# Token-mixing tails as two row tiles inside the next batch's score group, in a fused pooling attention and MLP-mixer kernel on Trainium2

## The chip, the cores and the metric

The kernel runs on one core of one Trainium2 chip. The metric is the device time of one execution in microseconds (us), given as the median of several runs. The engines are named as in the profile: PE is the matrix engine TensorE (PEld its weight loads), DVE is VectorE, ACT is ScalarE, POOL is GpSimd, SP is SyncE, which here only issues transfers.

## The reference

Inputs are q, k, v of 8 batches, 8 heads, 576 positions and 64 channels, and four weight matrices. What is computed, cut to what matters:

```python
k_p = k.reshape(B, H, Sp, pool, D).mean(axis=3)      # pool = 8, Sp = 72 keys
v_p = v.reshape(B, H, Sp, pool, D).mean(axis=3)
attn = softmax(q @ k_p.T / sqrt(D))
x = (attn @ v_p) as [B, 576, 512]
h = relu(x.T @ w_tok1) @ w_tok2                       # token mixing, 576 -> 256 -> 576
u = x + h.T
out = u + relu(u @ w_ch1) @ w_ch2                     # channel mixing, 512 -> 1536 -> 512
```

The kernel takes and gives float32; products are made in bf16.

## The kernel before, in words

The program is written as steps of batches (`2.s0` is step `s0` of batch 2) and units. A unit is the channel mixing of one batch's first 512 positions: unit n holds `l1_tile` (line 517: 12 tiles of four 512-column products, each emptied by a relu on ACT into `GT`, line 521) and then seven products of 12 matmuls with 256 columns (line 583), which a Strassen-like scheme makes out of sums of `GT` and `w_ch2` on DVE (`=1` to `=4`, lines 545 and 557; `w0` to `w3` once for the weights). There are nine units, one for each batch and a ninth for the remaining 64 positions (the tails) of all batches.

A unit yields 45 times: step numbers 0 to 23 lie after each two products of 512 columns, 24 to 44 after each four of 256 columns. The dictionary `PLAN[n]` says which steps of which batches are put in at each of these places, and so fixes the order on all engines: every engine works through its instructions in the order in which they are written. Up to the first unit the list `HEAD` does the same.

The steps of a batch b, with their lines:

- `lk`, `lq`, `lv`: loads of k, q and v, issued from the POOL queue (lines 118 and 128).
- `K0`, `K1`, `V0`, `V1`: pooling of k and v on POOL, three adds each (lines 174 to 180); `v1` is the same on DVE.
- `kpT`: four transposes of the pooled k on PE and a copy to `kD` on ACT (lines 222 and 224). `Q0`, `Q1`: transposes of q on DVE into `qD` (line 284).
- `s0`, `s1`, `s2`: a score group (`scores`, lines 297 and 306). The heads' products have 32 channels a piece, so four of them stand side by side on PE as 32-row tiles; two exponentials on ACT follow. `s0` and `s1` make 384 positions of one half of the heads each, `s2` the last 192 positions of all heads. They take both of the `p2` PSUM tiles.
- `av0` to `av4`: attention times pooled v, eight products (line 379), then a reciprocal and a multiplication on DVE (lines 383 and 384). `av0` to `av3` give 128 positions each into `x`, `av4` the last 64 into `xt`. An `xt` tile is shared by the two batches of a pair, batch 2i in its upper 64 rows and batch 2i+1 in its lower ones; `w_tok1` therefore stands with the tail's 64 rows twice, each time with zeros in the other half.
- `at0`, `at1`: the first token-mixing product, five products of 512 columns for each half of the 256 hidden rows (line 393), then a relu on ACT (line 395). The fifth product is that of the tail, with 64 of its 128 rows zero.
- `u0` to `u3`: the second token-mixing product and the residual, added on DVE (lines 415 and 416); `u4`: the tails of a pair of batches together (line 410), as one DVE add of 128 rows.
- `t0` to `t3` (PE), or `M0`, `M2`, `M4` (to DRAM), `M`, `MT` (back) and `T0` to `T5` (DVE transposes, line 458), bring `u` into the layout that the next unit needs.
- `g`: a gate (lines 716 and 717). DVE writes a flag and POOL copies it, so that POOL's later steps wait for DVE to come to that place; the next gate's write waits for the copy of the one before.

PSUM has four single banks (`p1a` to `p1d`), which `take` hands out in the order in which they were given back, and two double ones (`p2`). A product that takes a bank waits until its last content was read.

Of the kernel before, what the change touches and what calls it, by code (L numbers as in the profile page):

```python
# [8 lines left out]
FP32 = mybir.dt.float32  # L9
BF16 = mybir.dt.bfloat16  # L10
# [25 lines left out]
def kernel(  # L36
# [72 lines left out]
    exps = [singles.tile([SP, H * S + BP], BF16, name=f"ex{i}") for i in range(2)]  # L109
# [77 lines left out]
    def batch_steps(b):  # L187
# [101 lines left out]
        def scores(i):  # L289
            def go():  # L290
# [9 lines left out]
                exv = st["ex"][:, 0:H * S].rearrange("j (g a l n) -> j a l g n", g=2, a=2, l=2)  # L300
                for a in range(2):
# [23 lines left out]
        def avh(g, c):  # L325
            def go():
# [460 lines left out]
```

## Time and profile before

| | |
|---|---|
| time, median of 3 runs | 264.54 us (263.89 to 265.03) |
| profiled execution, its own time | 264.03 us |
| its span | 262.2 us |
| granted PE clock over the span | 1.00 |
| busy: PE, PEld | 255.8 us (98%), 160.4 us (61%) |
| busy: DVE, ACT, POOL | 179.7 us (69%), 119.2 us (45%), 150.0 us (57%) |
| DMA | 34.29 MB in 31704 packets, mean 131 GB/s |
| chain that ended last, by engine | PE 80%, POOL 8%, DMA 7%, DVE 3% |

The profile was taken from one execution. Its span runs from the first to the last instruction of the program. Groups of instructions are told by line, engine, operation and the tiles written and read. Ends of matmuls are modelled, so that a PE that shows no idle time may still have stood for a fraction of a microsecond; start times are measured. From the starts of the products of line 517, units 0 to 4 begin at 24.2, 56.5, 85.8, 113.5 and 143.8 us.

### The profile page before, as it was taken

What the parts mean: (1) busy time and instruction counts of PE and PEld (TensorE: products, weight loads), DVE (VectorE), ACT (ScalarE), POOL (GpSimd) and SP (SyncE); (2) the same over time, 40 slices, a digit from 0 to 9 for tenths busy, and PEclk for the clock granted to TensorE, in tenths of its full rate; (3) what the DMA queues carried; (4) which work ended last, traced back from release to release, by engine and by line L of the source; (5) the groups of instructions that cost most, each with busy time, mean ns of one, the idle gap of its engine ahead of it and who ended that gap; (6) DMA issues with size and microseconds to landing.
All of it is one profiled execution on the core that took longest, in us unless ns stands there. A gap on an engine that the chain in (4) does not pass through costs nothing.

```text
span 262.2 us, 5324 instructions
## 1 busy us (share of the span) xinstructions
PE 255.8 (98%) x2121; PEld 160.4 (61%) x2121; DVE 179.7 (69%) x370; ACT 119.2 (45%) x195; POOL 150.0 (57%) x177
## 2 busy tenths in 40 slices
PE   8899999999999999999999999999999999999994
PEld 3775556754658545864487448744774486486483
DVE  4566489998786657993899449964795486175183
ACT  2445754149465554435641584155535502612610
POOL 8576145999989999999939881988000000101000
PEclk9999999999999999999999999999999999999999
DMA  7999999992096839699357840831414054503204
GB/s 150 191 200 205 206 206 208 207 223 77 2 172 101 133 118 201 146 196 261 66 154 125 239 133 2 162 92 41 123 35 127 5 158 113 129 0 88 75 0 160
DMA packets 31704, 34.29 MB, mean 131 GB/s; under 512 B 3136, under 2 KB 23744, under 8 KB 31680
## 3 DMA queue, kind: packets, MB, share of 16 engines
q0 software_dynamic: 17632, 17.64, 42.6%
q1 hardware_dynamic: 13632, 15.93, 20.4%
q10 hardware_dynamic: 416, 0.39, 0.5%
q8 instruction: 16, 0.26, 0.4%
q14 instruction: 8, 0.07, 0.1%
HBM read 38.99 MB, written 12.58 MB: 197 GB/s over the span
## 4 chain that ended last, share of the span: by engine, by line
PE 80%; POOL 8%; DMA 7%; DVE 3%; issue 1%; POOLq 0%
PE p1d L517 9%; PE p1c L517 9%; PE p1a L517 8%; PE p1b L517 7%; PE p1b L583 7%; PE p1c L583 7%; PE p1a L583 6%; DMA qb<-in_q_dram 5%; PE p1d L583 4%; PE p L297 3%; PE p L379 3%; POOL t L174 2%; POOL t L175 2%; DMA kr<-in_k_dram 2%; PE p L583 2%; PE p1d L393 2%
## 5 line engine op out<-in xcount | busy, mean ns | idle before, releaser
L717 POOL COPY flag<-flag 1x1 f32<-1x1 f32 x47 | 12.6, 269 | 94.5 <-DVE flag L716 94.5
L517 PEld LDWEIGHTS <-w_ch 128*128 128x128 bf16 x432 | 39.6, 98 | 43.4 <-issue 1.8
L583 PEld LDWEIGHTS <-area 128*128 128x128 bf16 x432 | 40.9, 98 | 7.4 <-issue 1.2
L306 ACT ACTIVATE ex<-p 72x768 bf16<-72x768 f32 x42 | 31.6, 803 | 15.9 <-PE p L297 15.7
L583 PEld LDWEIGHTS <-GT 128*128 128x128 bf16 x324 | 30.8, 98 | 8.2 <-issue 2.4
L175 POOL TENSOR_TENSOR t<-t 72x512 f32<-72x512 f32 x23 | 31.0, 1346 | 1.8
L521 ACT ACTIVATE GT<-p1d 128x512 bf16<-128x512 f32 x29 | 17.3, 597 | 27.0 <-PE p1d L517 21.4
L517 PE MATMUL p1d<-uT,w_ch 128*128 128x512 bf16 x104 | 28.8, 379 | 0.0
L174 POOL TENSOR_TENSOR t<-kr 72x1024 f32<-72x1024 bf16 x12 | 25.9, 2155 | 0.5
L517 PE MATMUL p1c<-uT,w_ch 128*128 128x512 bf16 x96 | 26.1, 379 | 0.0
L521 ACT ACTIVATE GT<-p1b 128x512 bf16<-128x512 f32 x26 | 15.6, 598 | 23.2 <-PE p1b L517 16.8
L517 PE MATMUL p1a<-uT,w_ch 128*128 128x512 bf16 x92 | 25.3, 379 | 0.0
L517 PE MATMUL p1b<-uT,w_ch 128*128 128x512 bf16 x92 | 24.2, 379 | 0.0
L174 POOL TENSOR_TENSOR t<-vr 72x1024 f32<-72x1024 bf16 x11 | 24.1, 2187 | 0.3
L521 ACT ACTIVATE GT<-p1a 128x512 bf16<-128x512 f32 x26 | 15.5, 596 | 11.8 <-PE p1a L517 9.2
L521 ACT ACTIVATE GT<-p1c 128x512 bf16<-128x512 f32 x27 | 16.1, 598 | 8.7 <-PE p1c L517 8.3
L384 DVE TENSOR_TENSOR x<-p,den 128x512 bf16<-128x512 f32 x28 | 19.4, 692 | 1.0
L557 DVE TENSOR_TENSOR area<-GT 128x1536 bf16<-128x1536 bf16 x9 | 9.8, 1086 | 12.4 <-ACT GT L521 12.4
L545 DVE TENSOR_TENSOR area<-GT 128x1536 bf16<-128x1536 bf16 x9 | 10.6, 1178 | 10.1 <-ACT GT L521 7.7
L379 PEld LDWEIGHTS <-ex 72*128 72x128 bf16 x280 | 13.4, 98 | 5.6 <-DVE flag L716 0.4
L583 PE MATMUL p1c<-area,area 128*128 128x256 bf16 x120 | 15.4, 273 | 0.0
L379 PE MATMUL p<-vp,ex 72*128 72x65 bf16 x280 | 14.6, 194 | 0.0
(188 smaller groups left out, 461.1 us busy)
## 6 DMA issues: line engine op xcount, KB each, us to landing
out_dram<-o SPq DMA_DIRECT2D x32, 256.0 KB, 4.0
qb<-in_q_dram POOLq DMA_DIRECT2D x7, 576.0 KB, 9.3
kr<-in_k_dram POOLq DMA_DIRECT2D x7, 512.0 KB, 7.4
vr<-in_v_dram POOLq DMA_DIRECT2D x7, 512.0 KB, 9.8
w_ch<-in_moe_w_ch_dram POOLq DMA_DIRECT2D x5, 512.0 KB, 15.8
mem<-u SPq DMA_DIRECT2D x10, 256.0 KB, 2.0
v<-mem SPq DMA_DIRECT2D x20, 128.0 KB, 2.8
area<-in_q_dram SPq DMA_DIRECT2D x2, 288.0 KB, 3.0
```

The source lines that it names most:

```text
L174: eng.tensor_tensor(out=t4[:, 0:n], in0=t[:, hs, 0:4], in1=t[:, hs, 4:8], op=ALU.add)
L175: eng.tensor_tensor(out=t4[:, 0:n, 0:2], in0=t4[:, 0:n, 0:2], in1=t4[:, 0:n, 2:4], op=ALU.add)
L297: nc.tensor.matmul(out=pss[l // 2][0:SP, l % 2, o:o + n1 - n0], lhsT=st["kD"][quad, g, db, :], rhs=st["qD"][quad, g, n0:n1, db], start=(db ...
L306: nc.scalar.activation(out=dst, in_=src, func=AF.Exp, scale=scale)
L379: nc.tensor.matmul(out=ps[:, h // 4, (h % 4) * (D + 1):(h % 4 + 1) * (D + 1)], lhsT=st["ex"][:, h * S + n0:h * S + n0 + P], rhs=st["vp"][: ...
L384: nc.vector.tensor_tensor(out=dst.rearrange("p (a h d) -> p a h d", a=2, d=D), in0=view[:, :, :, 0:D], in1=den[rows, :, :, None].broadcast ...
L517: nc.tensor.matmul(out=ps, lhsT=w_ch1[:, kk, m * P:(m + 1) * P], rhs=uT[kk], start=(kk == 0), stop=(kk == 3))
L521: nc.scalar.activation(out=GT[:, m, :], in_=ps, func=AF.Relu)
L545: nc.vector.tensor_tensor(out=out, in0=a, in1=b, op=ALU.subtract)
L557: nc.vector.tensor_tensor(out=S4[:, 0], in0=GT[:, f, hi], in1=GT[:, sec, hi], op=ALU.add)
L583: nc.tensor.matmul(out=ps[i] if split else ps[:, i], lhsT=chunk(u, i, a(m)), rhs=w(m), start=start and m == 0 and (i == 0 or split), stop= ...
L717: nc.gpsimd.tensor_copy(out=flag[:, 1:2], in_=flag[:, 0:1])
```

## The change

For batches 2, 3 and 4 the tail's part of the first token-mixing product is taken out of `at0` and `at1` (four products then remain in each) and made as two products of 64 rows, one for each half of the hidden rows. They stand in the score groups `3.z1`, `4.z2` and `5.z0`, which are `s1`, `s2` and `s0` with the tails of the batch before behind their products, as two row tiles (rows 0 to 63 and rows 64 to 127 of PE), each into a bank of its own; `at0` and `at1` then add to these banks. For that the tail rows have to stand in both halves of `xt`: the exponentials of the last 64 positions are copied once more behind each head's 576 (an ACT copy after `s2`), so that `av4` works on 128 columns, the tail twice. Each batch has its own `xt` (`rests[b % 2]`), and `u4` adds the residual of a pair in two DVE instructions of 64 rows. Batches 0, 1, 5, 6 and 7 keep five products in `at0` and `at1`. The places of all steps in `PLAN` were set anew; apart from the three renamed groups and one more gate the steps are the same.

```diff
--- before.py
+++ after.py
@@ PLAN, units 0 to 4; the further ones are reordered in the same way @@
-    {0: "0.u3 1.Q0 2.lk 1.kpT", 3: "0.u1", 4: "1.s0 g g", 5: "1.Q1", 9: "1.s1 0.u0", 10: "1.vpool1 1.vpool0 g", 11: "1.s2", 12: "=3 0.u2 2.lq", 13: "1.av1", 14: "1.av3", 16: "1.av2", 18: "w0 3.lk", 19: "1.av0 3.lq", 20: "1.av4 w1 g", 23: "1.at1 2.lv", 24: "1.at0 3.lv =1", 25: "=2 =4", 26: "g", 28: "w3", 31: "1.u1 1.u2", 32: "1.t1", 33: "1.t2 w2", 34: "2.K0", 35: "1.u0", 38: "3.Q1 2.K1", 40: "1.u3", 41: "1.t0", 42: "g", 43: "2.Q0 1.t3", 44: "1.u4 2.V0 2.kpT"},
-    {2: "2.s0", 5: "2.Q1", 6: "2.s2", 9: "3.Q0 3.K0", 11: "3.K1", 12: "2.s1", 16: "2.v1", 17: "4.lq 2.av3 g", 18: "2.av2", 19: "2.av4", 22: "2.av1", 23: "2.av0 =1 =3", 24: "=2", 25: "4.lk g", 26: "g =4", 27: "3.kpT 5.lk 2.at0", 28: "g 3.s1 2.at1", 29: "3.V1", 30: "3.s2 2.u2", 32: "2.u3 3.s0", 33: "2.u0", 37: "2.t3", 39: "2.t0", 40: "2.u1 3.V0", 41: "4.Q1 2.t2", 42: "2.t1", 44: "4.lv"},
-    {2: "3.av4", 3: "3.av0 4.K0", 7: "3.av1", 8: "g 4.K1", 10: "3.av2 3.av3", 13: "g 3.at0", 14: "3.at1 g 6.lk", 16: "4.kpT", 17: "=3", 18: "4.Q0 3.u2", 19: "3.u1", 20: "3.u0", 21: "3.M0", 22: "3.u3 4.s2", 23: "3.M2 4.V1 3.u4", 24: "4.V0", 25: "=1", 26: "=2 3.M4", 27: "4.s0 g", 28: "6.lq", 30: "=4 g", 31: "4.s1 5.lv", 34: "3.M g", 35: "4.av2 3.T1", 36: "3.MT", 38: "3.T2", 40: "3.T3 3.T0", 41: "4.av4", 44: "5.lq 3.T5"},
-    {0: "5.K0 5.K1", 1: "4.av1", 4: "g", 6: "6.lv 4.av0", 7: "4.av3 5.Q0", 9: "5.V1 6.Q0", 10: "4.at1 4.at0", 12: "5.kpT", 13: "4.u2", 14: "4.u1", 15: "g", 16: "5.Q1 4.u3", 17: "5.s0", 19: "3.T4 =3", 21: "4.u0", 23: "=1", 25: "5.V0 4.M0", 26: "=2 5.s1", 27: "g", 29: "=4", 30: "5.s2", 31: "g", 33: "5.av2", 35: "5.av0 5.av1 4.M2 4.M", 39: "5.av3", 40: "4.T2 5.av4", 41: "4.T1", 42: "7.lq 4.T3", 43: "5.at0 4.T0", 44: "5.at1"},
-    {1: "6.K0", 2: "5.u2 5.u1", 4: "7.lk", 5: "6.K1", 6: "g", 7: "g 5.u3", 8: "6.kpT", 10: "5.u0", 13: "5.M2", 14: "6.s0", 15: "6.Q1", 16: "=3", 17: "6.V0", 18: "7.Q1", 23: "5.M0 5.M", 24: "6.V1 6.s1", 25: "=1", 26: "=2", 30: "=4 g", 31: "5.T0", 32: "g", 33: "7.Q0 6.s2", 34: "5.T2", 36: "6.av2", 38: "5.T3", 39: "5.T1", 41: "6.av3", 43: "5.u4", 44: "7.lv"},
...
+    {0: "1.kpT g", 3: "g", 4: "1.Q0", 6: "0.u2", 7: "1.s0", 8: "1.Q1 0.u0", 9: "2.lk", 10: "3.lq 0.u1 1.s1 1.vpool0", 11: "1.vpool1 =3 1.s2 0.u3", 12: "g", 13: "1.av1", 14: "1.av3", 15: "1.av2 2.lv", 17: "1.av0", 18: "w0", 19: "1.av4", 20: "2.lq", 21: "3.lk w1", 22: "g", 24: "=1 =2 3.lv", 25: "=4", 26: "1.at0 1.at1 g", 27: "w3 2.K0", 28: "1.u1", 31: "1.u2", 33: "1.t1 1.t2", 34: "w2", 36: "1.u0", 37: "3.Q1", 39: "1.u3", 41: "1.t0 2.K1", 42: "1.t3", 43: "2.Q0 1.u4", 44: "2.kpT"},
+    {0: "2.V0", 1: "2.s0 g", 4: "3.K1 3.K0 2.Q1", 6: "2.s2", 7: "2.v1", 8: "4.lq", 9: "g 5.lk 3.Q0", 12: "2.s1", 17: "2.av4", 19: "2.av1", 20: "2.av0", 22: "2.av3", 23: "2.av2 =1", 24: "4.lk g", 26: "3.kpT =3 =2", 27: "g =4", 28: "3.z1 2.at0 2.at1", 29: "3.s2 2.u3 2.u0", 30: "3.V1", 32: "g 2.u2", 34: "2.t3", 35: "3.s0 2.u1", 38: "2.t1", 40: "2.t0", 42: "2.t2", 43: "3.V0 3.av4", 44: "4.lv"},
+    {0: "4.K1", 1: "3.av0 4.Q0", 3: "4.K0 3.av2 g", 6: "3.av3", 7: "4.Q1", 8: "3.av1", 9: "g", 13: "6.lk", 14: "=3 g", 17: "4.V1", 20: "4.kpT", 21: "4.z2 3.at0", 22: "3.at1 4.s0 3.u2 3.u3", 23: "3.u1 3.u0 3.u4 =1", 25: "3.M2", 28: "=2 4.V0", 29: "4.s1 3.M0 3.M4", 30: "g", 31: "3.M =4", 32: "4.av3", 33: "4.av2", 37: "3.T2", 39: "3.T3 3.T0", 40: "3.T1", 41: "5.lv 4.av4 3.MT", 43: "6.lq", 44: "3.T5 4.av1 5.lq"},
+    {0: "5.K0 5.K1", 3: "4.av0", 8: "6.lv", 9: "5.V0 g", 10: "6.Q0 5.V1", 13: "5.kpT", 14: "3.T4", 15: "5.Q0", 17: "5.z0 4.at0", 18: "4.at1", 19: "=3", 20: "4.u0", 21: "5.Q1", 22: "4.u2 4.u1", 23: "4.u3 g", 24: "5.s1 =1", 26: "=2 4.M0", 29: "5.s2", 30: "g =4", 31: "g", 32: "5.av2 4.M2", 35: "5.av1", 36: "4.M", 37: "5.av3", 38: "5.av0", 40: "5.av4 4.T3 7.lq", 41: "4.T1", 42: "4.T2 4.T0", 43: "5.at0", 44: "5.at1"},
+    {2: "7.Q0", 3: "6.K1", 4: "5.u2 5.u3 5.u1", 7: "6.K0", 8: "5.u0", 10: "6.kpT 6.V1", 12: "5.M2 5.M0", 13: "5.M 6.s0 g", 16: "g", 19: "g =3", 21: "6.Q1 6.V0", 24: "7.Q1 =1", 25: "7.lk", 26: "=2", 27: "5.T2 6.s1", 28: "=4 5.T0 g", 32: "g", 33: "6.s2 7.lv", 41: "5.T3", 42: "5.T1", 43: "6.av3 5.u4", 44: "6.av1"},
...
@@ -106,7 +106,7 @@
 
 
     values = [singles.tile([SP, H, D + 1], BF16, name=f"vp{i}") for i in range(2)]
-    exps = [singles.tile([SP, H * S + BP], BF16, name=f"ex{i}") for i in range(2)]
+    exps = [singles.tile([SP, H, S + BP], BF16, name=f"ex{i}") for i in range(2)]
     rests = [singles.tile([P, DM], BF16, name=f"xt{i}") for i in range(2)]
     halves = [singles.tile([SP, H // 2, 4, D], FP32, name=f"t4_{i}") for i in range(2)]
     loaded = {}
@@ -192,7 +192,7 @@
 
         def prepare():
             kp = att.tile([SP, 2, 2, 4, D // 2], BF16, name="kp") if b >= 1 else None
-            st.update(kp=kp, vp=values[par], ex=exps[par], xt=rests[b // 2 % 2])
+            st.update(kp=kp, vp=values[par], ex=exps[par], xt=rests[b % 2])
             if not first:
                 st["kD"] = att.tile([P, 2, 2, SP], BF16, name="kD")
 
@@ -286,7 +286,7 @@
                     in_=pairs.rearrange("m (u r d) -> m u r d", u=2, d=D // 2))
             return go
 
-        def scores(i):
+        def scores(i, tail=False):
             def go():
                 pss = [ps_two.tile([P, 2, 512], FP32, name="p2") for _ in range(2)]
                 spans = [(i, 0, 0, S1)] if i < 2 else [(g, g * (S - S1), S1, S) for g in range(2)]
...
@@ -369,29 +373,35 @@
 
         def av(c):
             def go():
-                n0 = c * P if c < 4 else (8 * BP if par == 0 else 7 * BP)
-                rows = slice(0, P) if c < 4 else lower
-                n = rows.stop - rows.start
-                dst = late("x")[:, c, :] if c < 4 else st["xt"][rows, :]
+                dst = late("x")[:, c, :] if c < 4 else st["xt"]
                 den = outp.tile([P, 2, 4], FP32, name="den", bufs=4)
                 ps = ps_two.tile([P, 2, 512], FP32, name="p2")
                 for h in range(H):
                     nc.tensor.matmul(out=ps[:, h // 4, (h % 4) * (D + 1):(h % 4 + 1) * (D + 1)],
-                                     lhsT=st["ex"][:, h * S + n0:h * S + n0 + P], rhs=st["vp"][:, h, :],
+                                     lhsT=st["ex"][:, h, c * P:(c + 1) * P], rhs=st["vp"][:, h, :],
                                      start=True, stop=True)
-                view = ps[rows, :, 0:4 * (D + 1)].rearrange("p a (h e) -> p a h e", e=D + 1)
-                nc.vector.reciprocal(out=den[rows], in_=view[:, :, :, D])
+                view = ps[:, :, 0:4 * (D + 1)].rearrange("p a (h e) -> p a h e", e=D + 1)
+                nc.vector.reciprocal(out=den, in_=view[:, :, :, D])
                 nc.vector.tensor_tensor(out=dst.rearrange("p (a h d) -> p a h d", a=2, d=D),
                                         in0=view[:, :, :, 0:D],
-                                        in1=den[rows, :, :, None].broadcast_to([n, 2, 4, D]), op=ALU.mult)
-            return go
+                                        in1=den[:, :, :, None].broadcast_to([P, 2, 4, D]), op=ALU.mult)
+            return go
+
+        def at_tails():
+            st["at"] = [take([P, 512], FP32) for _ in range(2)]
+            for m in range(2):
+                half = slice(m * BP, (m + 1) * BP)
+                nc.tensor.matmul(out=st["at"][m], lhsT=w_tok1[half, 4 + m, m * P:(m + 1) * P], rhs=st["xt"][half],
+                                 start=True, stop=False, tile_position=(m * BP, 0), skip_group_check=True)
 
         def at(m):
             def go():
-                ps = take([P, 512], FP32)
-                for c in range(5):
-                    nc.tensor.matmul(out=ps, lhsT=w_tok1[:, c if c < 4 else 4 + par, m * P:(m + 1) * P],
-                                     rhs=st["x"][:, c, :] if c < 4 else st["xt"], start=(c == 0), stop=(c == 4))
+                early = "at" in st
+                ps = st["at"][m] if early else take([P, 512], FP32)
+                for c in range(4 if early else 5):
+                    nc.tensor.matmul(out=ps, lhsT=w_tok1[:, c, m * P:(m + 1) * P],
+                                     rhs=st["x"][:, c, :] if c < 4 else st["xt"], start=(c == 0 and not early),
+                                     stop=(c == (3 if early else 4)), skip_group_check=early)
                 nc.scalar.activation(out=late("AT")[:, m, :], in_=ps, func=AF.Relu)
                 give(ps)
                 tails[b // 2, par] = st["AT"]
@@ -410,7 +420,12 @@
                             nc.tensor.matmul(out=ps[half * BP:(half + 1) * BP], lhsT=w_tok2[:, m, 8 * BP:S],
                                              rhs=tails[b // 2, half][:, m, :], start=(m == 0), stop=(m == 1),
                                              tile_position=(0, half * BP), skip_group_check=True)
-                    x = st["xt"]
+                    for half in range(2):
+                        rows = slice(half * BP, (half + 1) * BP)
+                        nc.vector.tensor_tensor(out=rows_of(c)[rows], in0=blocked(ps[rows]),
+                                                in1=blocked(batches[b - 1 + half][2]["xt"][rows]), op=ALU.add)
+                    give(ps)
+                    return
                 for i, (w, a) in enumerate(mms):
                     nc.tensor.matmul(out=ps, lhsT=w, rhs=a, start=(i == 0), stop=(i == len(mms) - 1))
                 nc.vector.tensor_tensor(out=rows_of(c), in0=blocked(ps), in1=blocked(x), op=ALU.add)
@@ -491,7 +506,7 @@
                 name[f"kp{hp}"], name[f"kt{hp}"] = kp2(*hs), kt2(*hs)
             name[f"q{hp}"], name[f"o{hp}"], name[f"e{hp}"] = qT(hp), score(hp, 1), score(hp, 0)
         for i in range(3):
-            name[f"s{i}"] = scores(i)
+            name[f"s{i}"], name[f"z{i}"] = scores(i), scores(i, True)
         for c in range(5):
             name[f"av{c}"], name[f"u{c}"], name[f"t{c}"] = av(c), u(c), uT(c)
             for g in range(2):
@@ -503,7 +518,7 @@
         for i in range(3):
             name[f"M{2 * i}"] = spill(i)
         name["M"], name["MT"] = quads(0, 2), quads(2, 3)
-        name["at0"], name["at1"] = at(0), at(1)
+        name["at0"], name["at1"], name["tails"] = at(0), at(1), at_tails
         return prepare, name, st
 
 
@@ -746,8 +761,8 @@
         nc.vector.memset(w_tok1[:, 4:6, :], 0.0)
         for i in range(2):
             nc.vector.memset(values[i][:, :, D], float(POOL))
-            nc.vector.memset(exps[i][:, H * S:], 0.0)
-            nc.vector.memset(rests[i], 0.0)
+        nc.vector.memset(exps[0][:, :, S:], 0.0)
+        nc.vector.memset(rests[0], 0.0)
         for i, s in enumerate(HEAD.split()):
             if i == 3:
                 make_identity(nc, ident)
```

## The prediction

> **What bounds the kernel now.** I read the page's first part and the chain's shares, then the wait totals, then the timeline of TensorE for what a product costs, then the chain in order of time where it leaves TensorE, then VectorE and GpSimd there.
>
> The page, part 1 and part 4:
> ```profile
> PE 255.8 (98%) x2121; PEld 160.4 (61%) x2121; DVE 179.7 (69%) x370; ACT 119.2 (45%) x195; POOL 150.0 (57%) x177
> ...
> PE 80%; POOL 8%; DMA 7%; DVE 3%; issue 1%; POOLq 0%
> ```
> TensorE is the bound. From the start of unit 0 (24.2 us) it stops three times for 0.3 us or more, which I find by start-to-start times (a modelled end hides a short stop). Two are in unit 0, 0.30 us each, at 47.56 (a `u` product waits for a bank that VectorE has not emptied) and at 56.4 (`2.kpT` waits for GpSimd's second `kp`). The third is 0.61 us at 125.4. In the wait totals the third shows like this, with its cause on VectorE above it:
> ```profile
> DVE qD L284 <- DMA qb<-in_q_dram: 4.3, 1, 4.3
> ...
> PE p1c L415 <- DVE u L416: 0.4, 1, 0.4
> ```
> The chain in order of time there:
> ```profile
> 108.88 0.69 POOL qb L128
> 109.58 0.17 POOL flag L717
> 109.74 1.22 POOL vr L118 x2
> 110.97 0.12 POOL flag L717
> 111.08 12.19 DMA qb<-in_q_dram
> 123.27 0.02 issue
> 123.30 0.87 DVE qD L284 x2
> ...
> 125.40 0.59 PE p1c L415 x2
> 126.00 0.43 PE p1b L517 x2
> 126.43 0.46 PE p L297 x8
> ```
> Batch 5's q is the last of three loads that GpSimd issues together (`6.lq`, `5.lv`, `5.lq`). It lands at 123.27; VectorE, in order, has waited for it; batch 4's `u` adds queue behind. The score group that uses it, `5.s0`, starts at 126.43, 3.1 us after the landing, so TensorE itself never waits for that load. This cushion is what the new plan spends.
>
> **The change part by part.** Prices of TensorE from its timeline:
> ```profile
> 59.67 0.59 PE L517 MATMUL p1d<-uT,w_ch 128*128 128x512 bf16 x2
> 60.20 0.54 PE L297 MATMUL p<-qD,kD 32*72 32x192 bf16 x16
> 60.67 0.39 PE L517 MATMUL p1d<-uT,w_ch 128*128 128x512 bf16 x1
> ```
> A 512-column product takes 0.216 us in a stream (four in 0.86 in the chain). Two from 59.67 end at 60.10, the row tiles start at 60.20: an edge from full rows to row tiles costs 0.10. The group takes 0.47, of which four rounds of 192 columns are 0.32: 0.10 is the edge back and 0.05 lies inside.
>
> *Tails.* Removed: 2 x 0.216 = 0.43 for each of batches 2, 3, 4. Added to `3.z1`, `4.z2`, `5.z0`: two 64-row products side by side, 0.216, about 0.03 for a first round, and the edge from 32-row to 64-row tiles. No row shows that edge; it lies between 0 and the 0.10 of an edge to full rows, and I take 0.10, its nearest row. Sum 0.34, a gain of 0.09 each, 0.27 in all (0.57 with a free edge). If the two products ran one after the other it would be a loss of 0.12 each.
>
> [...]
>
> *Tail exponentials twice.* Seven ScalarE copies of 72x512. Nearest row: the 128x512 copy L425, 585 ns, so 4.1 us on an engine at 45%. Cover: four PSUM banks. In the densest stretch the relu of a tile whose products ended near 61.1 started at 62.20, and that bank is written again three tiles (2.6 us) after 61.1: about a microsecond is left, a copy takes half. I take 0; if the cover fails, up to 0.5 at such a place.
>
> *Batch pairs.* `u4` (batches 1, 3, 5, 7) becomes two VectorE adds of 64 rows. Halving the rows saves nothing (`xt` 64x512 takes 690 ns, `x` 128x512 takes 692), so VectorE gets four more adds of about 0.65 to 0.72. Start-up memsets: one 272 ns `xt` memset goes, a longer `ex` one comes, beside the wait for the first k: 0.
>
> *Gates and queues, unit 0.* Loads on GpSimd's queue move in order (`3.lq` before `2.lq`, `2.lk` later); all have over 5 us to their readers. The gate ahead of `2.K0` still follows the evictions of the first second-layer product, so `2.K1` still ends near 56 and `2.kpT` still waits about 0.3. `1.u2` again takes the bank of `1.u1`. 0, between -0.6 and +0.3. Unit 1: `3.kpT` comes one step earlier, within 0.3 us of `3.K0`'s end: 0 to 0.3.
>
> *Units 2 and 3, the large term.* Position of `5.z0`: unit 3 starts by the sum of TensorE's rows at 113.6 to 113.8 (113.51 before). In the old plan 18 steps of 0.432, three `av` (0.26 each), `4.at1`, `4.at0` (2.16), `kpT` (0.13) and three `u` (1.30) come first, plus the 0.61 stop: 126.3 (126.4 in the trace). In the new one only 18 steps, one `av` and `kpT` come first; `at` and `u` follow the group. TensorE is there at 121.7 to 121.9.
>
> Its data: `5.lq` is still the last of three, behind gate step 30 of unit 2. VectorE ahead of that gate, before:
> ```profile
> 102.78 0.74 DVE L416 TENSOR_TENSOR u_tails<-p1d,xt 128x512 bf16<-128x512 f32 x1 [0.84 <-PE p1d L410]
> 103.70 1.72 DVE L557 TENSOR_TENSOR area<-GT 128x1536 bf16<-128x1536 bf16 x1 [0.18 <-ACT GT L521]
> 105.34 0.68 DVE L626 TENSOR_TENSOR s<-p1c,u 128x512 f32<-128x512 f32 x1
> 105.94 1.43 DVE L545 TENSOR_TENSOR area<-area,GT 128x1536 bf16<-128x1536 bf16 x1
> 107.30 0.68 DVE L626 TENSOR_TENSOR o<-p1b,s 128x512 f32<-128x512 f32 x1
> 107.31 0.06 DVE L716 MEMSET flag<- 1x1 f32 x1
> ```
> After: the four `u` products now stand at steps 22 and 23, from 100.0; their adds run back to back from 100.5 at 0.65, the two `u_tails` adds to 104.4, then `=1` and `=2` at 0.87 (their spacing where GpSimd is quiet; 1.64 and 1.36 above, with GpSimd in `4.V0`), `s` and `o` at 0.63: the gate falls at 107.4. GpSimd should have finished `4.V0` by 105, as its batch 3 and 4 work starts earlier. Then flag copy (0.99 when it meets `=4`, as at 107.90), two `vr` issues (1.28), one `qb` (0.75): `5.lq` at 110.4, against 111.08. First issue 108.4; from first issue to last landing took 14.4 before, so it lands at 122.8 (119.7 by the median qb landing of 9.3). VectorE transposes for 0.78: `5.z0` at about 123.4, a stop of 1.5 us in plain view on TensorE. Behind it in TensorE's queue stands everything else; behind the transpose on VectorE `=3` and batch 4's `u` adds. The old 0.61 stop goes with it. The stop swallows what TensorE gained or lost before it, so the later half is fixed by the landing.
>
> *Later units.* `7.Q0` moves to step 2 of unit 4; `7.lq` is issued near 134 and took 5.7 us before: hidden. The other additional adds and moved spills have a unit or more to their readers: 0.1.
>
> Sum: -0.3 tails, -0.6 old stop, +1.5 new stop, +0 unit 0, less 0.1 of gain swallowed by the stop, +0.1 later = about +0.6 us. The profiled execution took 264.03 (span 262.2 and 1.8 around it), 0.5 under the median 264.54; on its own time that is 264.6, on the median 265.1. 0.5% of it, 1.3 us, is about what a measurement of this kernel can tell from no change.
>
> **The rivals.** (a) Slower: the sums meet GpSimd again as in the rows above, the gate slips by 1.3, `5.lq` issues near 111.7 and lands at 124.1; TensorE waits 2.9 and the sum is +2.0, 266.5. It decides from an issue later than about 111. For it: those rows, and stores that share the DMA engines after 117; against: GpSimd's earlier start. (b) Faster: the load lands as the median row, before 121; no stop, `2.K1` early too: -0.3 - 0.6 - 0.3 = -1.2, 263.3. For it the 9.3 median; against, this load is the third of its burst. (c) The tails don't run side by side: the first two lie ahead of the stop, so only batch 4's counts, 0.2 more than forecast: 265.3. All the gain of the change is then gone.
>
> **How the numbers follow.** Forecast 0.50, own range 264.0 to 266.0; (a) 0.25, (b) 0.17, (c) 0.08. Slower by over 0.5% takes most of (a), a fifth of the forecast and a little of (c): 0.36. Faster takes just over half of (b): 0.10. The range reaches into (b) and past (a): 263.5 to 267.0.
>
> **What would show it.** Right: about 0.34 us more in each z group, and both tail products starting within 0.01 us; TensorE idle ahead of `5.z0` (L297, near 122) released by L284, with a wait of L284 for qb above 2 us; the 125.4 stop gone. Wrong: no idle there and a qb landing before 121; the two 64-row products 0.2 us apart; stops of over 0.3 us in units 4 to 8, of which I see none.

## The result and the profile after

The changed kernel takes 266.11 us in the median (264.54 to 268.17, 22 runs), the kernel before on the same chip 264.70 (263.89 to 266.46, 22 runs): a ratio of 1.0058 [1.0034, 1.0082], slower by 0.6%. The profiled execution took 265.59 (span 263.8) against 264.03. The executions differ in the granted clock of TensorE: 15 of the 22 show a mean of 0.998 or more and a median of 265.59, the other 7 show 0.992 to 0.994 and take 267.3 to 268.17.

Page of the changed kernel, parts 1 and 4:

```profile
PE 255.3 (97%) x2097; PEld 160.2 (61%) x2121; DVE 181.0 (69%) x373; ACT 124.0 (47%) x202; POOL 151.2 (57%) x178
...
PE 90%; DMA 5%; DVE 2%; POOL 1%; issue 1%; DVEq 0%
```

TensorE has the same products (24 of their records are missing in this trace, while the 2121 weight loads are all there) and the span is 1.6 us longer, so it stands still more. The starts of the units (products of L532) say where:

| unit | 0 | 1 | 2 | 3 | 4 | 8 | last product |
|---|---|---|---|---|---|---|---|
| before | 24.18 | 56.51 | 85.76 | 113.51 | 143.75 | 239.02 | 258.46 |
| after | 24.01 | 56.42 | 85.75 | 114.20 | 145.27 | 240.60 | 260.04 |
| after less before | -0.17 | -0.09 | -0.01 | +0.69 | +1.52 | +1.58 | +1.58 |

All of it arises in units 2 and 3, a little over half in unit 3. The first product of unit 3, in TensorE's timeline, and VectorE's transposes of `u`, which this product reads:

```profile
113.70 0.42 PE L380 MATMUL p<-vp,ex 72*128 72x65 bf16 x8
114.20 1.02 PE L532 MATMUL p1c<-uT,w_ch 128*128 128x512 bf16 x3
```

```profile
113.07 1.08 DVE L473 STREAM_TRANSPOSE uT<-v 128x256 uint32<-128x256 uint32 x3
```

The eight attention products are done by 113.96 (8 x 0.033); TensorE stands 0.24 us until the transposes have ended at 114.15. In the kernel before they ended at 113.24, ahead of the unit's start. The wait totals name two more waits of TensorE that those of the kernel before do not have, and VectorE's wait above the first:

```profile
PE p L297 <- DVE qD L284: 1.7, 1, 1.7
...
PE p1b L222 <- POOL kp L178: 0.2, 1, 0.2
...
DVE qD L284 <- DMA qb<-in_q_dram: 3.8, 2, 3.6
```

The chain in order of time leads from the gate's copy on GpSimd to the score group `5.z0`:

```profile
108.55 0.83 POOL flag L732
109.38 1.23 POOL vr L118 x2
110.61 0.71 POOL qb L128
111.32 12.34 DMA qb<-in_q_dram
123.66 0.02 issue
123.69 0.79 DVE qD L284
124.47 0.14 issue
124.61 0.53 PE p L297 x8
```

In the kernel before this chain left the load for VectorE's `u` adds, and the score group came 3.1 us after the landing. Now the group follows within a microsecond of it. TensorE's timeline at that place (a matmul's end is modelled, so read the starts):

```profile
120.50 0.23 PE L222 MATMUL p1b<-ident,kp 72*128 72x72 bf16 x2
120.97 0.24 PE L222 MATMUL p1b<-ident,kp 72*128 72x72 bf16 x2 [0.24 <-POOL kp L178]
121.04 1.03 PE L532 MATMUL p1c<-uT,w_ch 128*128 128x512 bf16 x4
121.91 1.03 PE L532 MATMUL p1a<-uT,w_ch 128*128 128x512 bf16 x4
124.61 0.53 PE L297 MATMUL p<-qD,kD 32*72 32x384 bf16 x8 [1.68 <-DVE qD L284]
125.08 0.39 PE L394 MATMUL p1d<-xt,w_tok 64*128 64x512 bf16 x1
125.08 0.39 PE L394 MATMUL p1b<-xt,w_tok 64*128 64x512 bf16 x1
```

Four products from 121.91 end at 122.77 (4 x 0.216), with the edge to row tiles at 122.87: the stop is 1.74 us. The two transposes of `5.kpT` at 120.97 came 0.47 after the two before them instead of some 0.07, a stop of 0.40. The 0.61 stop that the kernel before had at 125.4 is gone, and from unit 4 on no stop over 0.3 us has been added.

VectorE ahead of the gate, the counterpart of the rows shown before:

```profile
103.42 1.46 DVE L425 TENSOR_TENSOR u_tails<-p1a,xt 64x512 bf16<-64x512 f32 x2
104.91 1.37 DVE L572 TENSOR_TENSOR area<-GT 128x1536 bf16<-128x1536 bf16 x1
106.31 0.69 DVE L641 TENSOR_TENSOR s<-p1b,u 128x512 f32<-128x512 f32 x1
106.92 0.95 DVE L560 TENSOR_TENSOR area<-area,GT 128x1536 bf16<-128x1536 bf16 x1
107.78 0.68 DVE L641 TENSOR_TENSOR o<-p1c,s 128x512 f32<-128x512 f32 x1
108.41 0.06 DVE L731 MEMSET flag<- 1x1 f32 x1
```

The change itself, in the undisturbed group `3.z1`, in TensorE's timeline:

```profile
72.21 0.53 PE L297 MATMUL p<-qD,kD 32*72 32x384 bf16 x8
72.68 0.39 PE L394 MATMUL p1d<-xt,w_tok 64*128 64x512 bf16 x1
72.68 0.39 PE L394 MATMUL p1a<-xt,w_tok 64*128 64x512 bf16 x1
73.00 1.04 PE L402 MATMUL p1d<-x,w_tok 128*128 128x512 bf16 x4
```

Both tail products start together. The 32-row group takes 0.47 up to them, as it took up to the next full product before, so its edge to 64-row tiles costs the same 0.10; from 72.68 to 73.00 is 0.32, one product of 0.216 and one more edge of 0.10. Unit 1, which holds this group, takes 29.33 us here and 29.44 in e1 below, the same order without row tiles.

### The profile page after: what moved, and what is told of

The parts are those of the page before. It is cut to its first block, busy times and chain, and to the rows that moved or that the text cites. A ratio compares the mean times of both kernels' runs of the same rounds, so it can differ in the third digit from the quotient of the medians.

```text
span 263.8 us, 5260 instructions
## 1 busy us (share of the span) xinstructions
PE 255.3 (97%) x2097; PEld 160.2 (61%) x2121; DVE 181.0 (69%) x373; ACT 124.0 (47%) x202; POOL 151.2 (57%) x178
## 4 chain that ended last, share of the span: by engine, by line
PE 90%; DMA 5%; DVE 2%; POOL 1%; issue 1%; DVEq 0%
PE p1b L532 9%; PE p1a L598 9%; PE p1c L532 9%; PE p1c L598 8%; PE p1d L532 8%; PE p1a L532 7%; PE p1b L598 6%; PE p1d L598 5%; DMA qb<-in_q_dram 5%; PE p L297 4%; PE p L380 3%; PE p1d L430 2%; PE p L598 2%; PE p1b L402 2%; PE p1a L402 1%; PE p1a L430 1%
## 5 line engine op out<-in xcount | busy, mean ns | idle before, releaser
L532 PEld LDWEIGHTS <-w_ch 128*128 128x128 bf16 x432 | 39.9, 98 | 44.0 <-issue 1.9
L732 POOL COPY flag<-flag 1x1 f32<-1x1 f32 x48 | 14.9, 310 | 88.2 <-DVE flag L731 88.1
L536 ACT ACTIVATE GT<-p1c 128x512 bf16<-128x512 f32 x29 | 17.3, 596 | 24.7 <-PE p1c L532 24.3
L536 ACT ACTIVATE GT<-p1b 128x512 bf16<-128x512 f32 x28 | 16.7, 597 | 25.7 <-PE p1b L532 15.6
L532 PE MATMUL p1c<-uT,w_ch 128*128 128x512 bf16 x101 | 27.8, 379 | 0.3
L532 PE MATMUL p1b<-uT,w_ch 128*128 128x512 bf16 x96 | 26.4, 379 | 0.2
L532 PE MATMUL p1d<-uT,w_ch 128*128 128x512 bf16 x90 | 24.1, 379 | 0.1
L532 PE MATMUL p1a<-uT,w_ch 128*128 128x512 bf16 x85 | 23.1, 379 | 0.2 <-issue 0.2
L536 ACT ACTIVATE GT<-p1d 128x512 bf16<-128x512 f32 x26 | 15.5, 598 | 8.3 <-PE p1d L532 8.2
L431 DVE TENSOR_TENSOR u<-p1d,x 128x512 bf16<-128x512 f32 x14 | 10.2, 729 | 12.4 <-PE p1d L430 11.8
L118 POOL DMA_DIRECT2D kr<-in_k_dram x17 | 11.0, 649 | 7.6 <-DMA w_ch<-in_moe_w_ch_dram 3.6
```

The costliest lines, as they stand in the source:

```text
L118: nc.gpsimd.dma_start(out=t[j0:j1, h0:h1].rearrange("j h i d -> j h (i d)"), in_=src[b, h0:h1].rearrange("h (j i) d -> j h (i d)", i=POOL) ...
L532: nc.tensor.matmul(out=ps, lhsT=w_ch1[:, kk, m * P:(m + 1) * P], rhs=uT[kk], start=(kk == 0), stop=(kk == 3))
L536: nc.scalar.activation(out=GT[:, m, :], in_=ps, func=AF.Relu)
L732: nc.gpsimd.tensor_copy(out=flag[:, 1:2], in_=flag[:, 0:1])
```

## The experiments

The theory: the row tiles do what they should, and the time is lost because `5.z0` stands ahead of the landing of batch 5's q. The rivals: the row tiles or the added ScalarE and VectorE work cost the time; or the new order costs it elsewhere. Edits are to entries of `PLAN` of the changed kernel if nothing else is said. Ratios are to the kernel before, from the same job.

**No row tiles (e1).** The order of the changed kernel, the tails back in `at0` and `at1`.

```diff
-28: "3.z1 2.at0 2.at1"    21: "4.z2 3.at0"    17: "5.z0 4.at0"
+28: "3.s1 2.at0 2.at1"    21: "4.s2 3.at0"    17: "5.s0 4.at0"
```

> The changed kernel with the three groups without the tails, and five products in each at again; plan, second exponentials and split adds stay. Theory (the group of batch 5 stands waiting for its q load): the 0.32 us that a group with tails takes against the 0.43 us removed are small and mostly swallowed by that wait, so this comes out within 0.3 us of the changed kernel, ratio to before 1.003 to 1.008, with a stop of about 1.5 us still ahead of the group. Rival (the row tiles themselves, their mode edges, cost the time): this falls back to the kernel before, ratio 0.998 to 1.002.

Measured: 265.91, 1.0047 [1.0017, 1.0077]. TensorE's timeline:

```profile
122.33 1.03 PE L532 MATMUL p1a<-uT,w_ch 128*128 128x512 bf16 x4
124.62 0.53 PE L297 MATMUL p<-qD,kD 32*72 32x384 bf16 x8 [1.26 <-DVE qD L284]
```

The group waits for q without row tiles too, for 1.33 us, and the time does not fall back to that of the kernel before: the rival is refuted. That the group starts within 0.01 us of the 124.61 of the changed kernel is chance. TensorE reaches it 0.42 later, but it is that much late from the start of unit 1 on (56.87 against 56.42), ahead of any row tile; q is issued 0.43 later as well, at 111.75, and lands after 11.92 us instead of 12.34. What the row tiles are worth ahead of a stop can't be read from this pair.

**New code, old plan (e2).** The changed kernel's functions with the whole `PLAN` of before, so without row tiles; the copied exponentials, `av4` on 128 columns and the two `u4` adds stay.

> The changed code (tail exponentials twice, an xt for each batch, u4 as two adds) with the plan of before and no row tiles. Theory: these additions are covered, ratio to before 0.999 to 1.002, the stop at 125.4 as in the kernel before. Rival (the copies on ScalarE and the additional adds on VectorE are what makes the change slower): 1 us or more over before, ratio 1.004 and up.

Measured: 264.98, 1.0019 [0.9996, 1.0041]. The added ScalarE and VectorE work costs at most about a microsecond by the interval, and no difference is resolved. It is not wholly covered under the old order: the trace has two stops for VectorE that the kernel before does not have, of 0.6 us at a score group (30.94) and 0.5 at the start of unit 7 (220.19), while the old stop at the `u` product is 0.43 instead of 0.61. With e1, which took the row tiles out, this leaves the order as the cause of the loss.

**Batch 5's q first (e3).** Batch 5's q is issued as the first of the three loads, batch 6's as the last; `6.Q0` moves behind `5.Q1`, so that VectorE doesn't wait for it.

```diff
-unit 2: 41: "5.lv 4.av4 3.MT", 43: "6.lq", 44: "3.T5 4.av1 5.lq"
-unit 3: 10: "6.Q0 5.V1", 21: "5.Q1"
+unit 2: 41: "5.lq 4.av4 3.MT", 43: "5.lv", 44: "3.T5 4.av1 6.lq"
+unit 3: 10: "5.V1", 21: "5.Q1 6.Q0"
```

> The changed kernel with batch 5's q loaded as the first of the three loads and batch 6's as the last, and 6.Q0 moved behind 5.Q1. Theory: q lands near 116, the stop ahead of the group of batch 5 is below 0.3 us, the time falls by 1.5 to 1.9 us against the changed kernel, ratio to before 0.995 to 1.000; kpT of batch 5 still waits 0.4 us for GpSimd. If long stops of TensorE are what lowers its granted clock in some executions of the changed kernel, every run here has clock 1.0. Rival (the group waits for something else, such as the keys or the PSUM tiles): the stop stays above 1 us.

Measured: 264.36, 0.9987 [0.9971, 1.0003]. TensorE's timeline:

```profile
120.73 0.24 PE L222 MATMUL p1b<-ident,kp 72*128 72x72 bf16 x2 [0.28 <-POOL kp L178]
120.80 1.03 PE L532 MATMUL p1c<-uT,w_ch 128*128 128x512 bf16 x4
121.67 1.03 PE L532 MATMUL p1a<-uT,w_ch 128*128 128x512 bf16 x4
122.63 0.53 PE L297 MATMUL p<-qD,kD 32*72 32x384 bf16 x8
```

The group follows 0.96 after the tile's start, 4 x 0.216 and an edge of 0.10: the stop is gone, and with it 1.75 us of the median. The order of three loads was the cause. The wait for the pooled k stays, at 0.45.

**The group later (e4).** The loads as in the changed kernel; batch 5's first group goes behind batch 4's `u` products, and its tails go back into `at`.

```diff
-17: "5.z0 4.at0", 23: "4.u3 g", 24: "5.s1 =1", 26: "=2 4.M0"
+17: "4.at0", 23: "5.s0 4.u3 g", 24: "=1", 26: "5.s1 =2 4.M0"
```

> The changed kernel with batch 5's first group as a plain one at step 23 of unit 3, behind at0, at1 and three u of batch 4, so that these five-product at fill the wait; two of the three pairs of row tiles are left. Theory: TensorE reaches the group after 126, the stop is gone, 1.4 to 1.9 us less than the changed kernel, ratio to before 0.995 to 1.001. Rival (the load's lateness comes back through VectorE, whose adds queue behind the transpose of q, as in the kernel before): a stop of 0.5 to 1 us at a u product, ratio 1.000 to 1.004.

Measured: 264.32, 0.9988 [0.9971, 1.0005]; the group starts at 129.00 with no stop there. Moving the consumer away cures it as well as moving the load forward.

**The same load in the kernel before (e8).** The same exchange in the kernel before, where this load made the 0.61 stop.

```diff
-unit 2: 28: "6.lq", 44: "5.lq 3.T5"    unit 3: 9: "5.V1 6.Q0", 16: "5.Q1 4.u3"
+unit 2: 28: "5.lq", 44: "6.lq 3.T5"    unit 3: 9: "5.V1", 16: "5.Q1 4.u3 6.Q0"
```

> The kernel before with the loads of batch 5's and batch 6's q exchanged and 6.Q0 behind 5.Q1. Theory: its 0.61 us stop at 125.4 came from the same load through VectorE; it goes, ratio to before 0.996 to 0.9995. Rival (the stop came from the order of VectorE's work, not from the load): the stop stays at 0.4 us or more, ratio 0.999 to 1.002.

Measured: 264.06, 0.9973 [0.9953, 0.9994]; no stop at the `u` products. Both plans had the same fault; the new one only laid it bare.

**K pooled earlier (e5).** Against the 0.40 wait of `5.kpT`: on GpSimd `5.lq`, `5.K0`, `5.lv`, `5.K1`, `6.lq`, so that the pooling begins before two of the loads are issued; `6.Q0` goes to place 29.

```diff
-unit 2: 41: "5.lv 4.av4 3.MT", 43: "6.lq", 44: "3.T5 4.av1 5.lq"
-unit 3: 0: "5.K0 5.K1", 10: "6.Q0 5.V1", 29: "5.s2"
+unit 2: 41: "5.lq 4.av4 3.MT", 44: "3.T5 4.av1"
+unit 3: 0: "5.K0 5.lv 5.K1 6.lq", 10: "5.V1", 29: "5.s2 6.Q0"
```

> As the run with batch 5's q first, and GpSimd pools batch 5's keys between the loads: 5.lq, K0, 5.lv, K1, 6.lq, with 6.Q0 at step 29 of unit 3. Theory (with q early the next thing late is the second key half, 0.4 us at kpT): that wait goes, K1 ends about 1 us earlier, 0.4 us less than with q first, ratio to before 0.995 to 1.000, no stop over 0.3 us in unit 3. Rival (the loads that are now later, 5.lv and 6.lq, become the next thing late, on GpSimd's V0 or VectorE's 6.Q0): a new stop of 0.5 us or more in the second half of unit 3 or in unit 4, ratio 1.000 to 1.005.

Measured: 264.06, 0.9985 [0.9965, 1.0005]. The wait for k is gone, but in the profiled execution two attention steps stand for 0.49 and 0.79 us, at 138.0 and 139.5, for PSUM that VectorE has not emptied: there, more than was won is given back within the unit. That execution took 265.18, 1.1 over the median, so how large the two stops are in the others is not shown.

**Batch 5's q first, batch 6's last (e9), and the same without row tiles (e10).** As e3, but `6.lq` after the pooling of k, and `6.Q0` at place 29; e10 changes the three groups in addition, as e1 does.

```diff
-unit 2: 44: "3.T5 4.av1 6.lq"    unit 3: 0: "5.K0 5.K1", 21: "5.Q1 6.Q0", 29: "5.s2"
+unit 2: 44: "3.T5 4.av1"    unit 3: 0: "5.K0 5.K1 6.lq", 21: "5.Q1", 29: "5.s2 6.Q0"
```

> The changed kernel with GpSimd's order 5.lq, 5.lv, K0, K1, 6.lq and 6.Q0 at step 29 of unit 3. Theory: q is early and the keys come 0.7 us earlier than in the run with q first, so neither the stop ahead of the group nor the 0.45 us at kpT is left, and the values are not put off as they were with the keys between the loads; 263.6 to 264.1 us, ratio 0.995 to 0.999. Rival (batch 6's q, now last, holds VectorE up at step 29): a stop of 0.5 us or more at a u or av step, ratio 0.999 to 1.003.

> The run with batch 5's q first and batch 6's last, without the tails in the groups (five products in each at). Theory: where no stop swallows it, the tails' gain of three times 0.11 us is seen in full: 0.3 us slower than with the tails, ratio 0.997 to 1.000, the last product of unit 8 starts 0.3 us later; the difference of the medians lies within the intervals. Rival (the row tiles cost something that the trace's starts do not show, such as clock): this is as fast or faster than with the tails.

Measured: 264.19, 1.0013 [0.9996, 1.0030], and 264.51, 1.0007 [0.9993, 1.0022]. In e9 no stop is left for q or k, but TensorE's timeline shows the next one:

```profile
138.60 0.43 PE L380 MATMUL p<-vp,ex 72*128 72x65 bf16 x8 [0.46 <-DVE x L385]
```

VectorE had `6.Q0` (0.77 at 133.71) in its densest stretch. The last product starts 0.44 later in e10 than in e9, but this is not the expected 0.33 of the row tiles: 0.30 of it lies ahead of unit 0 and 0.18 in unit 0, where there are none. The units with a pair of row tiles, each by one execution:

| unit | 1 | 2 | 3 | start of unit 1 to last product |
|---|---|---|---|---|
| with row tiles (e9) | 29.48 | 28.42 | 29.51 | 202.19 |
| without (e10) | 29.44 | 28.31 | 29.62 | 202.15 |

Unit 3 is 0.11 shorter with its pair, as one group's gain should make it. Unit 2 is 0.11 longer: in both runs unit 3 starts 0.05 us after VectorE's transposes of `u` have ended, so what its pair saves does not reach the unit's end (why VectorE ends later with it was not traced). Unit 1 of e9 is 0.14 longer than in the other runs with row tiles, so the 0.11 seen between the changed kernel and e1 is not seen here. The medians are 0.32 apart in the expected sense, the ratios 0.0006 in the other, and the intervals overlap. A net gain of the row tiles is not shown.

**`6.Q0` into the next unit (e12).** As e9, with `6.Q0` where VectorE has time.

```diff
-unit 3: 29: "5.s2 6.Q0"
+unit 3: 29: "5.s2"    unit 4: 6: "6.Q0"
```

> As the run with batch 5's q first and batch 6's last, and 6.Q0 at step 6 of unit 4, out of VectorE's dense stretch. Theory: the 0.62 us stop at an av step (its PSUM tile is emptied late by VectorE, which had 6.Q0 put in) goes and nothing takes its place: 263.2 to 263.8 us on a chip where the kernel before takes 263.9 to 264.7, ratio 0.995 to 0.999. Rival (the av step waits for something else, such as the values): the stop at 138.6 stays, ratio 0.999 to 1.003.

Measured: 263.58 (263.28 to 264.07, 12 runs) against 264.61, 0.9952 [0.9932, 0.9972]. TensorE's timeline:

```profile
120.44 0.29 PE L222 MATMUL p1b<-ident,kp 72*128 72x72 bf16 x4
120.57 1.03 PE L532 MATMUL p1c<-uT,w_ch 128*128 128x512 bf16 x4
121.43 1.03 PE L532 MATMUL p1a<-uT,w_ch 128*128 128x512 bf16 x4
122.39 0.53 PE L297 MATMUL p<-qD,kD 32*72 32x384 bf16 x8
```

No stop at k, at q or at the attention steps; the 0.24 us for VectorE ahead of unit 3 is still there. This order keeps all the row tiles and is faster than both kernels. How much of that the row tiles give is not shown: no run has this order without them, and the kernel before with its loads exchanged (e8, 0.9973) has an interval that overlaps with this one.

**Filling the stop (e6), lengthening it (e7), filling the long one (e11).** The rest of the question is the clock in 7 of 22 executions. e6 puts eight products (into a bank that is given back unread) ahead of `5.z0`; e7 issues `5.lq` behind `5.K0`, which lengthens the stop; e11 is e7 with 18 such products.

```diff
 e6:  -17: "5.z0 4.at0"    +17: "5.fill 5.z0 4.at0"
 e7:  -44: "3.T5 4.av1 5.lq"    +44: "3.T5 4.av1"
      -0: "5.K0 5.K1"    +0: "5.K0 5.lq 5.K1"
 e11: e7 and "5.fill 5.z0 4.at0", range(18)
+def fill():
+    ps = take([P, 512], FP32)
+    for _ in range(8):
+        nc.tensor.matmul(out=ps, lhsT=ident, rhs=w_ch1[:, 0, 0:512], start=True, stop=True)
+    give(ps)
```

> The changed kernel with eight more 512-column products, of no use, ahead of batch 5's group: 1.73 us of work in the place of the stop, so that TensorE never stands long. Theory A (two things: TensorE waits for q, and a stop of that length lets the granted clock fall in some executions): the undisturbed time stays that of the changed kernel within 0.3 us, no execution has a clock of 0.995 or less, and the median falls by about 0.5 us, to 265.0 to 265.8. Rival (the lower clock has nothing to do with the stop): about a third of the executions still show 0.992 to 0.994 and 267.3 to 268.2 us. If the group did not wait for a load but for work, the products would add their 1.7 us.

> The changed kernel with batch 5's q issued 4 us later, behind GpSimd's K0. [...] Rival (the clock falls for another reason): the time grows by the stop alone and the share of executions with a low clock stays near a third.

> The longer stop (q issued behind K0) with eighteen products of no use, 3.9 us, in its place. Theory: the time is that of the longer stop where the clock did not fall, 266.9 to 268.2 us, and no execution has a clock of 0.995 or less, against four of six. Rival (the clock falls for another reason than TensorE's idleness): half or more of the executions show 0.994 or less and 268.5 us or more.

Measured, e6: 265.99, 1.0051 [1.0024, 1.0077]. TensorE's timeline:

```profile
123.10 1.89 PE L400 MATMUL p1d<-w_ch,ident 128*128 128x512 bf16 x8
125.27 0.54 PE L297 MATMUL p<-qD,kD 32*72 32x384 bf16 x8 [0.28 <-DVE qD L284]
```

Eight more products cost the kernel nothing that the intervals show, since they lie in the wait. One of 12 executions shows a clock of 0.994 (268.16), against 7 of 22; but e1, with a stop of 1.3 us and no fill, has one of 12 too. The median did not come down as expected, and e6 does not settle the clock. The runs without the long stop say more: in e2 to e5, e8 to e10 and e12, whose profiles show no stop of TensorE over 0.8 us between the start-up and the last product, none of 95 executions has a clock under 0.997. Of 103 executions of the kernel before in the jobs of these runs one has 0.992 (268.65), so a low clock is rare without the long stop, not excluded.

e7: 268.96 (6 runs), 1.0156 [1.0112, 1.0200]. q landed at 126.44, the stop is 4.0 us, and 4 of 6 executions show a mean clock of 0.987 to 0.994. The profiled one is among them. Its windows (half a microsecond first, then 7 us each; busy time and count of PE, PEld, DVE, ACT, POOL, then the granted clock, the DMA share and GB/s) and TensorE's timeline:

```profile
125.50:126.00 0.50, 0.00 (x0) 0.00 (x0) 0.00 (x0) 0.00 (x0) 0.50 (x1) 0.95 1.22 224
126.00:133.00 7.00, 5.61 (x21) 1.93 (x22) 3.46 (x2) 2.10 (x3) 5.62 (x6) 0.52 0.32 54
133.00:140.00 7.00, 7.00 (x51) 3.98 (x48) 5.34 (x10) 3.78 (x6) 0.81 (x1) 1.00 0.17 61
```

```profile
122.39 1.03 PE L532 MATMUL p1a<-uT,w_ch 128*128 128x512 bf16 x4
127.39 0.86 PE L297 MATMUL p<-qD,kD 32*72 32x384 bf16 x8 [3.97 <-DVE qD L284]
...
128.72 1.89 PE L402 MATMUL p1d<-x,w_tok 128*128 128x512 bf16 x4
130.41 1.06 PE L532 MATMUL p1c<-uT,w_ch 128*128 128x512 bf16 x2
```

The last product ended at 123.26. The clock is halved (0.50 in the windows from 126.00 to 127.00) from 125.95 (0.95 as the mean of half a microsecond is half clock in its last 0.05) for 6.8 us: four products from 128.72 take 1.69, 0.42 each instead of 0.216. This stop thus costs a second time, after it has ended.

e11: 268.61 (5 runs), 1.0159 [1.0135, 1.0183]. All five clocks are 0.999 or 1.0, against 4 of 6 low ones in e7: with TensorE kept busy in the wait, the clock stayed. The time did not come down by as much as expected. The spans did more (median 266.3 against 267.2 in e7), but 1.8 to 2.8 us lay outside the span in e11, against 1.8 elsewhere, which I can't explain, and in the profiled executions VectorE got q 1.1 us earlier in e11 (125.36 against 126.47). For the fill as a remedy this settles nothing.

## Why the prediction was right or wrong

The predicted mechanism is what happened: `5.z0` ahead of the last load of the burst, the old cushion spent, TensorE in plain view. The measured 266.11 lies inside the range, 1.0 above the forecast and 0.1 above the forecast's own range; the rise of 0.6% falls just past the 0.5% that the forecast had stayed under. By rival (a)'s own condition, an issue later than about 111, it is (a) that took place: the issue was at 111.32. Of its price, +2.0, the profiled execution shows +1.56; by the medians at full clock the loss is 0.9, nearer to the forecast's +0.6. That the median of all 22 comes so close to (a)'s 266.5 is in part luck, since 0.5 of it is the lower clock, which no sum held. Point by point:

- **Tails.** Group with tails +0.32 (forecast 0.34), products removed 0.43: a gain of 0.11 each (0.09). The inner edge, taken from its nearest row, is 0.10. The forecast's 0.03 for a first round is seen in no run: one product of 0.216 and the edge make up the 0.32. Rival (c), products one after the other, is refuted by the equal starts. The sum counted all three gains but for 0.1. The trace shows 0.11 in unit 1, against e1; in unit 2 the wait for VectorE ahead of unit 3 takes it (28.45 with the pair, 28.33 in e1), and in unit 3 it shows only without the stop (e9 and e10).
- **Exponentials twice.** Seven copies at 618 ns instead of 585, cover intact, since no wait of TensorE for ScalarE stands in the totals; **`u4`** at 728 ns instead of 650 to 720. From the groups of instructions by line:

```profile
L310 ACT COPY ex<-ex 72x512 bf16<-72x512 bf16 x7 | 4.3, 618 | 0.2
L425 DVE TENSOR_TENSOR u_tails<-p1c,xt 64x512 bf16<-64x512 f32 x4 | 2.9, 728 | 0.3 <-PE p1c L420 0.3
```

- **Units 0 and 1** at nothing, within 0.1: right. **Later units** at 0.1: 0.06.
- **The large term, mis-sized.** The start of `5.z0` was put at 123.4 and measured 124.61; these 1.2 us are of the size by which the sum was missed (+1.56 against +0.6). Three quarters are the issue of `5.lq`, at 111.32 instead of 110.4, behind a gate at 108.41 instead of 107.4. The `u_tails` adds ended 0.5 late, and `=1` took 1.37 instead of 0.87; it began at 104.91, while GpSimd was in the last add of `4.V0` (to 105.47). That this overlap made it slower is argued from the rows before (1.72 and 1.43 beside `4.V0`) and after (0.95 for `=2`, with GpSimd idle), not tested. The step that failed was "GpSimd should have finished `4.V0` by 105": right within half a microsecond, on which another half hung. From the issue on it held: 12.34 to the landing. The rest is a slip in the sum (122.8 and 0.78 are 123.6) and the 0.14 between transpose and group. Another slip made the forecast smaller: the 0.1 of gain that the stop swallows was subtracted from the time, and with its sign put right the terms give +0.8.
- **Where TensorE stood meanwhile.** It came to the group at 122.8 instead of 121.7 to 121.9, which is why the stop is 1.74 and not more. Of this, 0.40 is the wait of `5.kpT`, which the sum left out: in the new plan `5.kpT` stands 6.3 us after the start of unit 3 instead of 8.6, and GpSimd, at the loads until 112.04, was done at 120.9. The rest is the start of unit 3, at 114.20 instead of 113.6 to 113.8. Unit 2 is 0.70 longer: an attention step that moved into it is 0.26 of that, the tails take 0.11 off, and TensorE stands 0.24 for VectorE's transposes at its end, a wait that the sum left out too. About 0.3 is left in three short stops beside the score groups (0.12 ahead of `4.z2` at 96.65, 0.07 and 0.09 behind the other two); what they wait for was not traced.
- **The clock, not in the sum.** In 15 executions at full clock the loss is 0.9 by medians (265.59 against 264.70); the other seven, some 2.35 slower, make it 1.4. That they are the ones in which the load lands later and the stop is longer is argued from e7, where a stop of 4.0 us and the half clock after it were seen; no trace of such an execution of the changed kernel was taken.

## What to carry to other kernels

When a consumer is moved forward in a fixed order, look up how long its data had lain there: that cushion, not the work that is saved, decides. Issue loads in the order of their first use, and after each cure ask what is late next; here it was q, then the pooled k, then PSUM that VectorE had to empty, and only when all three were met was the new order faster than the kernel before by more than its interval. A saving of 0.11 us in a group is no saving of the kernel until the next thing that TensorE waits for comes as much earlier: compare units between two runs, not the starts of the last product, in which the start-up of each execution stands too. A load in the bound engine's view must be costed with its gate, and a gate's time with what works beside the operations in front of it (here `=1` took 1.37 us with `4.V0` beside it, `=2` 0.95 with GpSimd idle).

## What the runs showed of the hardware

A stop of TensorE can cost more than its length. In e7, with a stop of 4.0 us, the clock was halved 2.7 us after the last product and stayed so for 6.8 us, 5.4 of them after work had begun again. In the profiled execution of the changed kernel a stop of 1.74 us left it at 1.00.

Half clock for 6.8 us of e7's span of 269.1 us makes a mean of 0.987 (1 less 0.5 x 6.8 / 269.1), an estimate from its windows, and 0.987 is the mean that this execution shows. The seven slower executions of the changed kernel show 0.992 to 0.994; none of them was traced.
